# Another split of the first loads over two DMA queues, in a fused linear-attention and MLP kernel

## The chip, the cores and the metric

The kernel runs on one core of a Trainium2 chip. The metric is device time in microseconds (us) of one execution, as the median over several runs. A core has five engines that run their own instruction lists side by side and wait for each other through semaphores: TensorE (PE in the profile, with PEld for its weight loads), VectorE (DVE), ScalarE (ACT), GpSimd (POOL) and SyncE (SP). Data comes from the chip's main memory (HBM) into on-chip memory (SBUF) by DMA: an engine issues a DMA instruction, and 16 DMA engines, shared by all, move the bytes in packets. In this kernel DMAs are issued by POOL (the profile's queue q0, "software_dynamic") and by SP (queue q1, "hardware_dynamic").

## The reference

Eight batches of eight heads, 576 positions, head size 64. Attention with a cosine-weighted feature map, and then a two-layer MLP with a squared ReLU:

```python
theta = np.pi / 2.0 * pos / S
phi(x) = concat([relu(x) * cos(theta), relu(x) * sin(theta)], axis=-1)
q_p, k_p = phi(q), phi(k)
kv = einsum('bhsf,bhsd->bhfd', k_p, v)
z = sum(k_p, axis=2)
num = einsum('bhsf,bhfd->bhsd', q_p, kv)
den = einsum('bhsf,bhf->bhs', q_p, z)[..., None] + 1e-06
x = (num / den) with the heads side by side     # 4608 tokens x 512
h = x @ w_in                                    # 512 x 2048
out = (relu(h) ** 2) @ w_out                    # 2048 x 512
```

All inputs and the output are float32. The matmuls run in bf16.

## The kernel before

A batch has 576 positions. The first 512 are the "main" part: 128 partitions with four positions (j = 0 to 3) each, all heads, 1 MB in float32. The last 64 are the "tail": they are loaded with two DMAs of 64 KB, one for each half of the heads, onto the two halves of the partitions. `load` (lines 61 to 75) issues both, and `piece` (81) gives the part that belongs to a step j; step 4 is the tail. A tile of each of k, v, q and of each tail exists twice (`bufs=2`), so two batches may be on the chip.

For one batch the work is this. `att_k` (192) makes the feature map of k into `kp` (cosine half on VectorE, line 173; sine half on ScalarE, line 183; both scale by columns `cos_col` and `sin_col`). `att_v` (196) casts v to bf16 into `vext`, which has a column of ones so that z comes out of the same matmul. `att_kv` (224) multiplies k by v over all steps (`kz`, line 243). `att_feat` makes the feature map of q (`qp`), `att_qT_pe` (278) transposes it on TensorE (`tq`), `att_num` (301) multiplies it by kv, `att_div` (320) divides, giving x, and `att_x_pe` (349) transposes x. Then `gemm1` (367) multiplies by w_in (`hps`, line 388) in slots, ScalarE applies the ReLU (396), VectorE squares (403), and `gemm2` or `pair_mm` multiplies by w_out.

The order on each engine is written out by hand, inside `tc.manual_schedule()` (742): batch 0's attention stands first by itself, and from line 785 on the slots of the MLP run, with pieces of the next batches' attention hung onto slot numbers (`at`, `plan`). Each engine works through its own list in order. TensorE is kept busy from the start by `warm(34)` (747): 34 matmuls on a tile of zeros, whose result nobody reads; `warm(1)` (770) and `fill` stand further on.

The first loads, in the order of the code: k of batch 0 on POOL with its two tails on SP; `constants()` (92), which on POOL makes an index (`iota`, 99) and the identity matrix and on ScalarE two sine activations for `sin_col` and `cos_col`; v on POOL with its tails on SP; q on POOL in two halves (steps 0 and 1, then 2 and 3) with its tails on SP. Behind the work of batch 0 in the code, but with nothing to hold them on POOL, follow w_in in four pieces (`load_w1`, 117; float32 in HBM, cast to bf16 on the way; piece i holds what slot i of `gemm1` needs), q of batch 1 with its tails, a piece of w_out, k of batch 1, a piece of w_out, v of batch 1, two pieces of w_out, and batch 2.

The scheduler gives POOL's DMAs eight semaphores in turn. A ninth DMA waits at issue until the one that had its semaphore before has landed, and what stands behind it in POOL's list waits too. In the program before, the eight first are k, v, the halves of q and the four pieces of w_in; the next, q of batch 1, waits for k.

Of the kernel before, what the change touches and what calls it, by code (L numbers as in the profile page):

```python
# [11 lines left out]
F32 = mybir.dt.float32  # L12
# [7 lines left out]
def kernel(  # L20
# [9 lines left out]
    nc = tc.nc  # L30
    P = nc.NUM_PARTITIONS
    B, H, S, D = q.shape
# [6 lines left out]
    J = S // P  # L39
    MAIN = J * P  # L40
    TAIL = S - MAIN
    HH = H // 2
# [5 lines left out]
    inp = ctx.enter_context(tc.tile_pool(name="inp", bufs=2))  # L48
# [9 lines left out]

    kqv = {}

    def load(src, nm, b, eng, parts=1, tail_eng=None):
        main = inp.tile([P, H, J, D], F32, name=nm, tag=nm, bufs=2)
        tail = inp.tile([P, HH, D], F32, name=nm + "t", tag=nm + "t", bufs=2)
        for i in range(parts):
            js = slice(i * J // parts, (i + 1) * J // parts)
            eng.dma_start(
                out=main[:, :, js, :],
                in_=src[b, :, 0:MAIN, :].rearrange("h (p j) d -> p h j d", j=J)[:, :, js, :],
            )
        for g in range(2):  # L70
            (tail_eng or eng).dma_start(
                out=tail[g * TAIL : (g + 1) * TAIL, :, :],
                in_=src[b, g * HH : (g + 1) * HH, MAIN:S, :].rearrange("h p d -> p h d"),
            )
        kqv[nm, b] = (main, tail)

    def load_batch(b, eng, order):
        for nm in order:
            load({"k": k, "v": v, "q": q}[nm], nm, b, eng)

    def piece(nm, b, j):
        main, tail = kqv[nm, b]
        return main[:, :, j, :] if j < J else tail[:, :, :]


    ident = const.tile([P, P], BF16, name="ident")
# [5 lines left out]
    def constants():  # L92
        sidx = const.tile([P, J + 1], F32, name="sidx")
        for p0, p1, c, n, base, mult in [
            (0, P, 0, J, 0, J),
            (0, TAIL, J, 1, MAIN, 1),
            (TAIL, P, J, 1, MAIN, 1),
        ]:
            nc.gpsimd.iota(
                sidx[p0:p1, c : c + n],  # L100
                pattern=[[1, n]],
                base=base,
                channel_multiplier=mult,
                allow_small_or_imprecise_dtypes=True,
            )
        bias_pi2 = const.tile([P, 1], F32, name="bias_pi2")
        nc.vector.memset(bias_pi2, math.pi / 2.0)
        theta_scale = (math.pi / 2.0) / S
        nc.scalar.activation(cos_col, sidx, ACTF.Sin, bias=bias_pi2[:], scale=-theta_scale)
        nc.scalar.activation(sin_col, sidx, ACTF.Sin, bias=0.0, scale=theta_scale)  # L110
        make_identity(nc, ident)
# [5 lines left out]
    def load_w1(i, n):  # L117
        f0, f1 = i * DFF // n, (i + 1) * DFF // n
        nc.gpsimd.dma_start(
            out=w1sb[:, :, f0:f1],  # L120
            in_=moe_w_in[:, f0:f1].rearrange("(kb p) f -> p kb f", p=P),
        )

    def load_w2(i, n):
        h0, h1 = i * HB // n, (i + 1) * HB // n
        nc.gpsimd.dma_start(
            out=w2sb[:, h0:h1, :],
            in_=moe_w_out[h0 * P : h1 * P, :].rearrange("(hb p) f -> p hb f", p=P),
        )
# [62 lines left out]
    def att_k(b, j, cos=feat_cos):  # L192
        for f in (cos, feat_sin):
            f(kp_of(b, j), piece("k", b, j), j)

    def att_v(b, j, eng, h0=0, h1=H):
        copy = eng.copy if eng is nc.scalar else eng.tensor_copy
        vx, vxt = vexts[b % 2]
        if j == J:
            copy(out=vxt[:, :, 0:D], in_=piece("v", b, j))  # L200
        else:
            copy(out=vx[:, j, h0:h1, 0:D], in_=piece("v", b, j)[:, h0:h1, :])  # L202

    def warm(n):

        wm = ps_h.tile([P, 2, FP], F32, name="wm", tag="hps", bufs=2)
        for i in range(n):
            nc.tensor.matmul(
                out=wm[:, i % 2, :], lhsT=zeros[:, 0:P], rhs=zeros[:, :], start=True, stop=True
            )  # L210
# [13 lines left out]
    def att_kv(b, part):  # L224
        vx, vxt = vexts[b % 2]
        if part == 0:
            kvzs[b] = att.tile([P, H, E1], BF16, name="kvz", tag="kvz", bufs=2)
            kzs[b] = ps_a.tile([P, 2, FP], F32, name="kz", tag="pa", bufs=1)
        kz = kzs[b]

        for j in (0, 1) if part == 0 else range(2, NS):
            for hh in range(HH):
                for half in range(2):
                    h = half * HH + hh
                    if j < J:
                        lhsT, rhs = kp_of(b, j)[:, h, :], vx[:, j, h, :]
                    else:  # L240
                        p0, p1 = half * TAIL, (half + 1) * TAIL
                        lhsT, rhs = kp_of(b, j)[p0:p1, hh, :], vxt[p0:p1, hh, :]
                    nc.tensor.matmul(  # L243
                        out=kz[:, half, hh * E1 : (hh + 1) * E1],
                        lhsT=lhsT,
                        rhs=rhs,
                        start=(j == 0 and hh == 0),
                        stop=(j == J and hh == HH - 1),
                    )
        if part == 1 and b:  # L250
            att_kvz(b, nc.scalar.copy)

    def att_kvz(b, copy):
        copy(
            out=kvzs[b].rearrange("p (a h) e -> p a (h e)", a=2),
            in_=kzs[b][:, :, 0 : HH * E1],
        )

    def att_feat(b, j, parts="cs"):
        for c in parts:  # L260
            f = feat_cos if c == "c" else feat_sin
            f(qp_of(b, j), piece("q", b, j), j)
# [15 lines left out]
    def att_qT_pe(b, j, apart=False):  # L278

        nh = H if j < J else HH  # L280
        tq = ps_y.tile([P, H, P], BF16, name="tq", tag="yps", bufs=2)
        tqs[b, j] = [tq[:, 0:HH, :]]
        if apart:
            hi = ps_h.tile([P, HH, P], BF16, name="tqh", tag="hps", bufs=2)
            tqs[b, j].append(hi)
        elif nh == H:
            tqs[b, j].append(tq[:, HH:H, :])
        for h in range(nh):
            nc.tensor.transpose(  # L289
                tqs[b, j][h // HH][:, h % HH, :], qp_of(b, j)[:, h, :], ident[:, :]  # L290
            )

    def att_qT_copy(b, j, both=False):
        qpTs[b, j] = []
        for i, tq in enumerate(tqs[b, j]):
            t = att.tile([P, HH, P], BF16, name=f"qpTp{i}", tag=f"qpTp{i}", bufs=3)
            copy = nc.scalar.copy if both and i else nc.vector.tensor_copy
            copy(out=t[:, :, :], in_=tq[:, :, :])
            qpTs[b, j].append(t)
# [363 lines left out]
    for j in (2, 3):  # L663
# [12 lines left out]
        k=(8, 8, 8, 9, 9),  # L676
        f=(4, 5, 6, 12, 13),
        v=(10, 10, 10, 10, 10),
        kv=(11, 11),
        d=(12, 14, 16, 17, 20),  # L680
        t=(5, 6, 7, 16, 19),
# [7 lines left out]
        k=(21, 22, 23, 24, 25),  # L689
# [8 lines left out]
        k=(29, 31, 32, 34, 35),  # L698
# [5 lines left out]
    for b in range(4, B):  # L704
# [5 lines left out]
            k=(o, o, o + 1, o + 1, o + 2),  # L710
# [29 lines left out]
            fn2(*args)  # L740

    with tc.manual_schedule():
        load(k, "k", 0, nc.gpsimd, 1, nc.sync)
        constants()
        load(v, "v", 0, nc.gpsimd, 1, nc.sync)
        load(q, "q", 0, nc.gpsimd, 2, nc.sync)
        warm(34)
        for j in range(NS):
            att_k(0, j)
        att_v(0, 0, nc.vector)  # L750
        att_v(0, 1, nc.scalar)
        att_v(0, 2, nc.vector)
        att_v(0, 3, nc.vector)
        att_v(0, J, nc.vector)
        for i in range(4):
            load_w1(i, 4)
        load_batch(1, nc.gpsimd, "q")
        load_w2(0, 4)
        load_batch(1, nc.gpsimd, "k")
        load_w2(1, 4)  # L760
        load_batch(1, nc.gpsimd, "v")
        for i in range(2, 4):
            load_w2(i, 4)
        load_batch(2, nc.gpsimd, "qkv")
        att_kv(0, 0)
        att_kv(0, 1)
        att_feat(0, 0)
        att_feat(0, 1)
        att_kvz(0, nc.vector.tensor_copy)
        warm(1)  # L770
        for j in range(2):
            att_qT_pe(0, j, True)
        for j in range(2):
            att_qT_copy(0, j, True)
            att_num(0, j, True)
        for j in range(2):
            att_div(0, j)
        att_feat(0, 2, "s")
        att_feat(0, 3, "s")
        for j in range(2):  # L780
            fill(4 - j)
            att_x_pe(0, j, True)
        att_feat(0, 2, "c")
        att_feat(0, 3, "c")
        for s in range(len(slots)):
            run(s)
# [29 lines left out]
```

## Time and profile before

| | |
|---|---|
| median of 6 runs | 289.0 us (288.72 to 290.7) |
| profiled execution, its own time | 289.09 us |
| its span in the profile | 287.3 us |
| busy share of the span: PE, PEld, DVE, ACT, POOL | 97%, 82%, 71%, 56%, 15% |
| chain that ended last | PE 89%, DMA 3%, DVE 2%, ACT 2% |
| read from HBM, written | 36.70 MB, 9.44 MB |
| SP's first DMA issue, POOL's | 0.74 us, 1.29 us |
| warm(34) | 1.19 to 11.04 us |
| first kz matmul, first tq, first hps | 12.36, 14.06, 18.25 us |
| granted TensorE clock, mean | 0.997 |

Times inside the run count from the start of the span. A line of the timeline gives the start, the time taken, the engine, the line of the code, the operation with the tile written and the tiles read, and in brackets how long the engine had been idle and what ended that. "xN" says that N instructions are merged into the line. A DMA instruction's own time is only that of its issue; when the data has landed is seen from who was waiting for it.

### The profile page before, as it was taken

Reading aid. Unit: us, or ns where it says so; the run is one execution under the profiler, and the core shown is the slowest. Engines: PE = TensorE matmul, PEld = TensorE weight load, DVE = VectorE, ACT = ScalarE, POOL = GpSimd, SP = SyncE. Lnnn points to the kernel's source line nnn. Section 1 sums busy time; section 2 is a strip of 40 time slices with the busy share of each in tenths; the row PEclk is TensorE's granted clock in tenths of the full one; section 3 lists DMA queues with packets and bytes.
Section 4 is the critical chain, followed back from the end, with each engine's and each line's share of the span. In section 5 each row is a group of like instructions: output and inputs, shape, how many; then the busy total and the mean of one; then the engine's idle time right before and its main releaser. Section 6 shows DMA issues by size and latency. Waiting matters only on the chain.

```text
span 287.3 us, 7337 instructions
## 1 busy us (share of the span) xinstructions
PE 279.9 (97%) x3070; PEld 235.9 (82%) x3070; DVE 204.6 (71%) x457; ACT 161.7 (56%) x245; POOL 42.1 (15%) x70
## 2 busy tenths in 40 slices
PE   8899999999999999999999999999999999999995
PEld 3479845888678888889988888888988888889884
DVE  0767664688698499787598776977677877546585
ACT  2675743579759769445881448834695461155210
POOL 8633506650000000000002000000000000000002
PEclk9999999999999999999999999999999999999998
DMA  6999995999468899999429985499809620300014
GB/s 184 334 206 289 323 264 201 364 363 276 76 99 205 184 258 229 234 327 186 147 95 205 344 158 164 124 252 285 230 3 232 118 46 3 141 7 2 0 75 146
DMA packets 74497, 53.04 MB, mean 185 GB/s; under 512 B 52032, under 2 KB 68928, under 8 KB 74464
## 3 DMA queue, kind: packets, MB, share of 16 engines
q1 hardware_dynamic: 63840, 26.09, 40.2%
q0 software_dynamic: 10480, 26.35, 30.2%
q8 instruction: 24, 0.39, 0.6%
q10 hardware_dynamic: 144, 0.13, 0.1%
q14 instruction: 9, 0.07, 0.1%
HBM read 36.70 MB, written 9.44 MB: 161 GB/s over the span
## 4 chain that ended last, share of the span: by engine, by line
PE 89%; DMA 3%; DVE 2%; ACT 2%; issue 1%; POOL 1%; POOLq 0%; ACTq 0%
PE hps L388 42%; PE ya L530 9%; PE yc L530 9%; PE yu L530 7%; PE yv L530 5%; PE num L315 4%; PE kz L243 3%; DMA v<-in_v_dram 3%; PE yps L461 2%; PE yps L437 2%; PE yh L437 2%; PE tq L289 1%; DVE ysb L542 1%; DVE u L542 1%; PE tx L356 1%
## 5 line engine op out<-in xcount | busy, mean ns | idle before, releaser
L388 PEld LDWEIGHTS <-w1sb 128*128 128x128 bf16 x1344 | 113.4, 98 | 12.4 <-issue 2.0
L388 PE MATMUL hps<-xT,w1sb 128*128 128x256 bf16 (+1 forms) x1088 | 119.3, 266 | 0.7 <-ACT rt L396 0.2
L396 ACT ACTIVATE rt<-hps 128x1024 bf16<-128x1024 f32 x72 | 73.6, 1023 | 67.1 <-PE hps L388 44.8
L403 DVE TENSOR_TENSOR gT<-rt 128x1024 bf16<-128x1024 bf16 x64 | 44.0, 687 | 20.1 <-ACT rt L396 20.1
L530 PEld LDWEIGHTS <-gs 128*128 128x128 bf16 x480 | 46.8, 98 | 5.4
L415 POOL DMA_DIRECT2D out_dram<-ysb x14 | 7.5, 539 | 171.6 <-DVE ysb L542 144.9
L530 PEld LDWEIGHTS <-gT 128*128 128x128 bf16 x312 | 29.8, 98 | 3.5
L183 ACT ACTIVATE kp<-k,sin_col 128x512 bf16<-128x512 f32 x32 | 22.4, 717 | 4.3 <-DMA k<-in_k_dram 4.3
L329 DVE TENSOR_TENSOR x<-num,rden 128x512 bf16<-128x512 f32 x32 | 22.1, 691 | 1.1
L183 ACT ACTIVATE qp<-q,sin_col 128x512 bf16<-128x512 f32 x32 | 22.0, 720 | 0.8 <-DMA q<-in_q_dram 0.8
L325 DVE TENSOR_SCALAR den<-num 128x8 f32<-128x8 f32 (+1 forms) x40 | 6.6, 164 | 21.2 <-PE num L315 21.1
L526 DVE TENSOR_TENSOR gs<-gT 128x1024 bf16<-128x1024 bf16 x26 | 17.8, 685 | 0.0
L530 PE MATMUL ya<-w2t,gs 128*128 128x256 bf16 x120 | 15.6, 273 | 0.0
L530 PE MATMUL yu<-w2t,gs 128*128 128x256 bf16 x120 | 15.6, 273 | 0.0
L530 PE MATMUL yc<-w2sb,gs 128*128 128x256 bf16 x120 | 15.6, 273 | 0.0
L388 PE MATMUL hps<-xTt,w1sb 128*128 128x128 bf16 x256 | 15.1, 219 | 0.2 <-ACT rt L396 0.2
L173 DVE TENSOR_SCALAR kp<-k,cos_col 128x512 bf16<-128x512 f32 x21 | 10.7, 533 | 6.1 <-DMA k<-in_k_dram 6.1
L173 DVE TENSOR_SCALAR qp<-q,cos_col 128x512 bf16<-128x512 f32 x32 | 15.0, 495 | 0.1
L202 ACT CAST vext<-v 128x512 bf16<-128x512 f32 x23 | 14.1, 614 | 1.4 <-DMA v<-in_v_dram 1.4
L530 PE MATMUL yu<-w2sb,gs 128*128 128x256 bf16 x112 | 14.5, 273 | 0.0
L581 ACT COPY s<-yu 128x256 f32<-128x256 f32 x14 | 5.2, 372 | 15.3 <-PE yu L530 15.3
L530 PE MATMUL yc<-w2sb,gT 128*128 128x256 bf16 x104 | 13.5, 273 | 0.0
(98 smaller groups left out, 338.6 us busy)
## 6 DMA issues: line engine op xcount, KB each, us to landing
out_dram<-ysb POOLq DMA_DIRECT2D x14, 512.0 KB, 4.2
k<-in_k_dram POOLq DMA_DIRECT2D x4, 1024.0 KB, 8.0
v<-in_v_dram POOLq DMA_DIRECT2D x4, 1024.0 KB, 8.7
k<-in_k_dram SPq DMA_DIRECT2D x4, 1024.0 KB, 7.2
v<-in_v_dram SPq DMA_DIRECT2D x4, 1024.0 KB, 8.5
q<-in_q_dram SPq DMA_DIRECT2D x4, 1024.0 KB, 5.8
q<-in_q_dram POOLq DMA_DIRECT2D x3, 1024.0 KB, 12.2
w1sb<-in_moe_w_in_dram POOLq DMA_DIRECT2D x4, 512.0 KB, 13.7
```

Source lines behind the costliest of these rows:

```text
L173: nc.vector.tensor_scalar(out=dst[:, :, 0:D], in0=src, scalar1=0.0, scalar2=cos_col[:, j : j + 1], op0=ALU.max, op1=ALU.mult,)
L183: nc.scalar.activation(out=dst[:, :, D:F], in_=src, func=ACTF.Relu, scale=sin_col[:, j : j + 1])
L202: copy(out=vx[:, j, h0:h1, 0:D], in_=piece("v", b, j)[:, h0:h1, :])
L243: nc.tensor.matmul(out=kz[:, half, hh * E1 : (hh + 1) * E1], lhsT=lhsT, rhs=rhs, start=(j == 0 and hh == 0), stop=(j == J and hh == HH - 1),)
L315: nc.tensor.matmul(out=out, lhsT=lhsT, rhs=kvz[:, half * HH + hh, :], start=True, stop=True)
L329: nc.vector.tensor_tensor(out=x_of(b, j).rearrange("p (b k) (l d) -> p b k l d", b=n, l=2), in0=n4[:, :, :, 0:D].rearrange("p b (k l) d -> ...
L388: nc.tensor.matmul(out=out, lhsT=w1sb[:, kb, hb * P : (hb + 1) * P], rhs=rhs, start=(kb == 0), stop=(kb == KB - 1),)
L396: nc.scalar.activation(out=rt[:, :, :], in_=hps[:, :, :], func=ACTF.Relu)
L403: nc.vector.tensor_tensor(out=dst, in0=rt[:, :, :], in1=rt[:, :, :], op=ALU.mult)
L437: nc.tensor.matmul(out=ypss[b][tt], lhsT=gTs[b][:, hb, tt * P : (tt + 1) * P], rhs=w2sb[:, hb, :], start=(hb == 0), stop=(hb == HB - 1),)
L526: nc.vector.tensor_tensor(out=t[:, :, :], in0=in0, in1=in1, op=op)
L530: nc.tensor.matmul(out=acc, lhsT=lhs[:, hb, :], rhs=rhs[:, hb, :], start=(hb == 0), stop=(hb == HB2 - 1),)
```

## The change

`load` is split in two: `load_main` for the first 512 positions and `load_tail` for the last 64, each with one queue. `load_batch`, which serves batches 1 to 7, calls both in turn and issues what it issued before. For batch 0 the order of the first loads is new:

- k's main part is issued by SP, and nothing else is: the six tail DMAs that SP had are gone from its list.
- POOL issues k's tail (two DMAs), v, v's tail (two), then makes its part of the constants, and then issues the halves of q.
- q's tail (two DMAs) is issued by POOL behind the four pieces of w_in and ahead of q of batch 1.
- `warm(34)` becomes `warm(31)`.

With the eight semaphores in turn, POOL's first eight DMAs are now k's two tails, v, v's two tails, the halves of q and the first piece of w_in. The second and the third piece of w_in wait for k's tails, the fourth for v, the two tails of q for v's tails, and q of batch 1 for the first half of q. The compute instructions of VectorE and ScalarE are the same, in the same order; TensorE's list loses three warm matmuls.

```diff
-    def load(src, nm, b, eng, parts=1, tail_eng=None):
+    def load_main(src, nm, b, eng, parts=1):
         main = inp.tile([P, H, J, D], F32, name=nm, tag=nm, bufs=2)
-        tail = inp.tile([P, HH, D], F32, name=nm + "t", tag=nm + "t", bufs=2)
         for i in range(parts):
             js = slice(i * J // parts, (i + 1) * J // parts)
             eng.dma_start(
                 out=main[:, :, js, :],
                 in_=src[b, :, 0:MAIN, :].rearrange("h (p j) d -> p h j d", j=J)[:, :, js, :],
             )
+        kqv[nm, b] = main
+
+    def load_tail(src, nm, b, eng):
+        tail = inp.tile([P, HH, D], F32, name=nm + "t", tag=nm + "t", bufs=2)
         for g in range(2):
-            (tail_eng or eng).dma_start(
+            eng.dma_start(
                 out=tail[g * TAIL : (g + 1) * TAIL, :, :],
                 in_=src[b, g * HH : (g + 1) * HH, MAIN:S, :].rearrange("h p d -> p h d"),
             )
-        kqv[nm, b] = (main, tail)
+        kqv[nm + "t", b] = tail
...
     with tc.manual_schedule():
-        load(k, "k", 0, nc.gpsimd, 1, nc.sync)
+        load_main(k, "k", 0, nc.sync)
+        load_tail(k, "k", 0, nc.gpsimd)
+        load_main(v, "v", 0, nc.gpsimd)
+        load_tail(v, "v", 0, nc.gpsimd)
         constants()
-        load(v, "v", 0, nc.gpsimd, 1, nc.sync)
-        load(q, "q", 0, nc.gpsimd, 2, nc.sync)
-        warm(34)
+        load_main(q, "q", 0, nc.gpsimd, 2)
+        warm(31)
...
         for i in range(4):
             load_w1(i, 4)
+        load_tail(q, "q", 0, nc.gpsimd)
         load_batch(1, nc.gpsimd, "q")
```

More of the change, by code (lines that the diff above doesn't have):

```diff
@@ L74, in load @@
             )
-        kqv[nm, b] = (main, tail)
+        kqv[nm + "t", b] = tail
     def load_batch(b, eng, order):
         for nm in order:
-            load({"k": k, "v": v, "q": q}[nm], nm, b, eng)
+            for part in (load_main, load_tail):
+                part({"k": k, "v": v, "q": q}[nm], nm, b, eng)
     def piece(nm, b, j):
-        main, tail = kqv[nm, b]
-        return main[:, :, j, :] if j < J else tail[:, :, :]
+        return kqv[nm, b][:, :, j, :] if j < J else kqv[nm + "t", b][:, :, :]
     ident = const.tile([P, P], BF16, name="ident")
```

## The prediction

> **What bounds the kernel now.** Read first the page: PE is busy 97% of the span and holds 89% of the chain that ended last, so a gain must come from the head, where the tensor engine is not yet fed. Read next the chain of waits in order of time; columns are start, length (us) and what:
>
> ```profile
> 3.51 8.34 DMA v<-in_v_dram
> ...
> 11.87 0.44 DVE vext L202
> ...
> 12.36 1.36 PE kz L243 x40
> 13.72 0.32 PE wm L208
> ...
> 14.06 0.40 PE tq L289 x4
> ```
>
> The head waits for v to land at 11.85, casts it, multiplies k by v (kz), then transposes q (tq). The ScalarE timeline (start, length, operation, in brackets the idle time before it and its releaser) shows that three landings stand close together:
>
> ```profile
> 7.55 2.56 ACT L183 ACTIVATE kp<-k,sin_col 128x512 bf16<-128x512 f32 x4 [4.27 <-DMA k<-in_k_dram]
> 11.87 0.62 ACT L202 CAST vext<-v 128x512 bf16<-128x512 f32 x1 [1.36 <-DMA v<-in_v_dram]
> 13.29 1.33 ACT L183 ACTIVATE qp<-q,sin_col 128x512 bf16<-128x512 f32 x2 [0.79 <-DMA q<-in_q_dram]
> ```
>
> k lands at 7.5, v at 11.85, the first half of q at 13.27; tq starts 0.77 after q, and kz with one warm matmul ends at the same moment (14.04). So v and q bind together, k has slack. What sets the landings is read from the DMA view of 4 to 12 us (queue, packets, MB, share of 16 engines):
>
> ```profile
> q0 software_dynamic: 643, 2.47, 85.3%
> q1 hardware_dynamic: 1087, 0.26, 14.8%
> ```
>
> The shares sum to 100%: the engines are full, so bytes in front decide. q0 is POOL's queue, q1 SP's. After the head, the w_in pieces bind almost as hard (POOL and PE timelines):
>
> ```profile
> 25.08 0.76 POOL L126 DMA_DIRECT2D w2sb<-in_moe_w_out_dram  x1 [1.92 <-DMA w1sb<-in_moe_w_in_dram]
> 25.14 1.03 PE L388 MATMUL hps<-xT,w1sb 128*128 128x256 bf16 x8
> ```
>
> POOL was released by the fourth w_in piece at about 25.05, and PE's first matmul on it starts at 25.14.
>
> **The change, part by part.** *Prices of bytes.* On q0, 85.3% of 8 us is 6.82 us for 2.47 MB: 0.362 MB per us. So a 1.05 MB main takes 2.90 us, half of q 1.45. On q1 the four tail DMAs of v and q took 14.8% of 8 us, 1.18 us: 0.59 for a pair of tails (0.13 MB), where q0's rate would take 0.36. A main on q1 is seen at 205.2 to 207.2 us: 0.75 MB at a 106.4% share, 2.13 us, so 2.98 us for k.
>
> *Bytes before the first half of q.* Before: k 2.90, v 2.90, half q 1.45, three pairs of tails 1.77, sum 9.02 us. After: k 2.98, v 2.90, half q 1.45, two pairs of tails on POOL 0.72, sum 8.05, since q's tail goes behind w_in. That is 0.97 less. The start of the stream stays: SP's first issue is at 0.74 in both, and the first packets come at 2.2. From 2 to 4 us the share is 57.6%, so of the 1.8 us after 2.2 some 0.65 stay empty; a quiet main on SP (203.7 to 205.2) fills 60.9%, leaving 0.59, and now k's tail (0.36) falls into that hole. I take 0.3 for it, bounds 0 and 0.36. q moves by 0.97 + 0.3 = 1.27, to 12.0; tq by the same, to 12.79. Bounds: if tails cost on POOL what they cost on SP (0.59), 0.5; if the start-up hole closes wholly (0.65), 1.6.
>
> *v and kz.* In front of v's end: before 2.90 + 2.90 + 1.77 = 7.57, after 2.98 + 2.90 + 0.36 = 6.24, so v moves by 1.33 + 0.3 = 1.6, to 10.25. kz starts 0.49 later (12.36 against 11.87), 10.74, ends 12.10, and with the warm matmul 12.44: 0.35 before q lets tq go. q decides.
>
> *warm 34 to 31.* Three warm matmuls at 0.213 us end the block at 10.40 instead of 11.04. I cost this at nothing: kz is hidden behind q. With 34, kz would run 11.04 to 12.40 and tq could go at 12.74, still under 12.79. If that cover is gone, it is worth 0.3.
>
> *k alone on SP.* One issue replaces six (SP's next work is at 62.9), and starts 0.55 before POOL's did. The quiet case at 202.55 landed 5.4 us after issue, which gives 6.1; the median of k on SP, 7.2 us with its own tails and other traffic, gives 7.9. What follows k on VectorE: four kp (2.78) and kpt, casts 3.07 after the landing, 1.34 of casts, then qp and 0.77 to tq: k's landing + 5.2. To stay behind q's 12.79, k must land by 7.6. I take 6.1 because k is on the engines alone at first; with 7.9 the gain shrinks to 0.9.
>
> *POOL's order.* POOL's first DMA starts at 1.29. Now two kt issues (1.25), v (0.94), two vt (1.25), and 0.15 because a first issue took 1.05 and not 0.90: 4.88. The constants follow, which took 2.35 to 3.49: the last iota ends at 5.40, the cosine table 0.33 later, the sine table at 5.83. kp needs them; k's landing at 6.1 hides them by 0.3. q's halves issue at 6.05, 1.6 later than at 4.46. POOL's first k packets came at 3.0, 1.7 after issue, so q's can come at 7.75, while v's bytes last until about 9: hidden, with 1.3 to spare. The w_in pieces issue at 7.8 to 10.15 for three of them; POOL keeps eight DMAs in flight, and with four tails among them the fourth piece waits for v's landing, 10.25, where it went at 8.4. Queued behind it are q's two tails, q of batch 1, the w_out pieces and batch 1's k and v. Three w_in pieces of 2.55 us (the spacing of their landings: 17.3, 19.95, 22.5, 25.05) and q are ahead in the stream, so it is covered for over 8 us.
>
> *What is late next.* The w_in pieces move by the same 1.27 as q, and PE by 1.27: the 0.09 us of margin at 25.14 stays, and caps the gain at what the stream gives. Behind w_in, q's tails add 0.36, so q of batch 1 comes 0.9 earlier only: it released POOL at 27.93, PE's need (VectorE qp at 28.75) moves by 1.27, and 0.4 of slack is left. q's own tail is read at 40.69. From 18.25 PE runs without a wait of length (after 40 us the list of waits gives it 0.4 us), so the shift passes to the end.
>
> *Sum.* Span 287.3 - 1.27 = 286.03. Outside the span lie 289.09 - 287.3 = 1.79: 287.82. The profiled run stands 0.09 above the median 289.0, so 287.7 is my number; bounds 0.5 and 1.6 give 287.4 to 288.5.
>
> **A rule against it.** Rows first: while both queues were flowing the engines gave each about as many packets, whatever their size. From 8.5 to 11.5 us (256-byte tails against 4-KB packets), and from 164.25 to 165.25 (v's 1-KB packets on SP against the result's on POOL):
>
> ```profile
> q0 software_dynamic: 265, 1.02, 92.3%
> q1 hardware_dynamic: 249, 0.06, 9.2%
> ```
>
> ```profile
> q0 software_dynamic: 81, 0.33, 80.9%
> q1 hardware_dynamic: 80, 0.08, 21.9%
> ```
>
> But where SP's DMA was under way first, POOL's barely came through, at 157 to 159.5:
>
> ```profile
> q1 hardware_dynamic: 500, 0.51, 79.2%
> q0 software_dynamic: 23, 0.04, 4.3%
> ```
>
> and 580 against 28 at 6.5 to 7.25. The Trainium skill, "DMA: Bandwidth & Descriptors", section "Queues, rings and completion order", says that each engine takes turns between the queues it has work for, a packet at a time. By that rule alone k would get a fifth of the bytes once v starts, and the sum would be the first rival's, 294.0. The last two rows differ from the rule, and k starts before v, so I forecast by them, but not by much.
>
> **The rivals.** *First, slower: k is outrun on its own queue.* v's packets can come from 2.69 + 1.7 = 4.4. By then k has had 2.2 us: 0.27 MB in the first 1.5 (seen at 203.7 to 205.2), then 0.25, less up to 0.13 for its tail: 0.39 to 0.52. The rest, 0.53 to 0.66 MB, at the 0.08 MB per us of 164.25, takes 6.6 to 8.2 us, and POOL has v, v's tail and q (2.2 MB at 0.33, 7 us) and then w_in to keep it up. k lands at 11.0 to 12.6, say 11.9; tq at 17.1, 3.0 late. Also PE idles from 10.4 until k + 3.5 = 15.4, 5 us. At the end the granted clock was at 0.5 some 2.1 us after the last matmul (283.8), and at the start warm matmuls were 0.43 apart until 5.9, 4.7 us after the first. PE's pieces of the chain in such a stretch (kz, warm, tq, num, fills) are about 4 us; doubled they add 0 (hidden) to 4: 2. Sum: 289.0 + 3.0 + 2 = 294.0, bounds 291 to 297. It decides from a k landing past 8.9 (14.06 - 5.2).
>
> The Trainium skill, "TensorE: Matmul & The Clock Gate", section "Part 1: The HAM clock gate", puts the relapse at an idle window of about 3.4 us; no idle stretch of PE inside this trace is that long, so it shows neither for nor against (after the warm block the idle time is 1.32).
>
> *Second, no change: shared halfway.* POOL's packets stay scarce for 1 us (as at 6.5 to 7.25) and then go one for one: k has 0.2 to 0.33 MB left at 5.4, 2.5 to 4.1 us more, landing 7.9 to 9.5, tq 13.1 to 14.7: 288.0 to 289.6, 288.8 in the middle. For it: both kinds of rows occur. Against: v's and k's tails arrive on POOL ahead and open its queue at 2.8.
>
> **How the numbers follow.** Forecast 0.58, first rival 0.32, second 0.10. A difference under 0.3% (0.87 us: 288.1 to 289.9) can't be told from none. Of the forecast, 0.05 lies above 288.1. Faster 0.53, same 0.15, slower 0.32. The likeliest case's own range is 287.4 to 288.5. The whole range goes from 287.2 (0.03 below) to 294.0, which leaves half of the first rival out: 0.19 outside.
>
> **What would show it.** Right: kp starts at about 6.1, vext at 10.3, tq at 12.8, the first hps at 17.0, w_in's pieces 1.3 earlier each. Wrong: kp starts after 8.9, v lands before k, and in 4.4 to 10 us the two queues show like numbers of packets; then the warm block is followed by a PE gap of over 3 us. If q lands at 12 but hps does not move, w_in held it.

## The result, and the profile after

| kernel | median us | runs | ratio to before (95%) |
|---|---|---|---|
| before | 289.07 (288.66 to 290.7) | 48 | |
| changed | 287.92 (287.21 to 294.24) | 22 | 0.996 [0.9949, 0.997] |

The change is worth 1.15 us, 0.4%; the interval goes from 0.3% to 0.5%. Two executions of the changed kernel were disturbed (294.24 us, and the first profiled one with 294.11) and are left out of the ratio, so the lines below are from another execution of the same program (`again`: 288.01 us, span 286.2). The page's line numbers have moved by 3 against before.

ScalarE's timeline in the head (start, length, operation, idle time before and its releaser) is read against the three landings shown of before, 7.55, 11.87 and 13.29:

```profile
6.24 2.56 ACT L186 ACTIVATE kp<-k,sin_col 128x512 bf16<-128x512 f32 x4 [0.47 <-DMA k<-in_k_dram]
9.48 0.62 ACT L205 CAST vext<-v 128x512 bf16<-128x512 f32 x1 [0.28 <-DMA v<-in_v_dram]
10.98 1.34 ACT L186 ACTIVATE qp<-q,sin_col 128x512 bf16<-128x512 f32 x2 [0.88 <-DMA q<-in_q_dram]
```

All three are earlier: k by 1.31, v by 2.39, q by 2.31. The DMA view of 2 to 4 us and then of 4 to 8 us shows where that comes from (queue, packets, MB, share of the 16 engines). First before:

```profile
q1 hardware_dynamic: 540, 0.13, 28.8%
q0 software_dynamic: 27, 0.11, 28.8%
```

and the changed kernel in the same 2 us:

```profile
q1 hardware_dynamic: 488, 0.50, 90.4%
```

By 4 us 0.50 MB have moved instead of 0.24; by 8 us, with 1.55 against 1.29 MB more, the lead is 0.52 MB. SP's queue carries k's first packets at 1.86 and the engines are full from 3 us on (104% from 3 to 4), while POOL's k came in at 3.2.

The end moved by less than the head. TensorE's timeline shows what took the place of the landing of q:

```profile
11.76 0.40 PE L292 MATMUL tq<-ident,qp 128*128 128x128 bf16 x4 [0.29 <-ACT qp L186]
...
16.56 1.96 PE L391 MATMUL hps<-xT,w1sb 128*128 128x128 bf16 x32 [0.45 <-DMA w1sb<-in_moe_w_in_dram]
...
21.59 1.92 PE L391 MATMUL hps<-xT,w1sb 128*128 128x256 bf16 x16 [0.19 <-DMA w1sb<-in_moe_w_in_dram]
...
24.20 1.92 PE L391 MATMUL hps<-xT,w1sb 128*128 128x256 bf16 x16 [0.22 <-DMA w1sb<-in_moe_w_in_dram]
```

The first tq is 2.30 us earlier (14.06 before), the first hps 1.69 (18.25), the fourth slot's hps only 0.94 (25.14). In between, the tensor engine now waits three times for w_in; before it waited for it not once. The chain of waits (start, length, what) says the same: it no longer runs over v and kz, but over POOL's issues and the landing of the fourth w_in piece (the 13.61 us are its time in the queue behind q and the three pieces ahead of it).

```profile
5.97 2.02 POOL q L65 x2
8.00 2.54 POOL w1sb L122 x3
10.54 13.61 DMA w1sb<-in_moe_w_in_dram
24.20 1.92 PE hps L391 x16
```

One figure makes all later runs readable: from the fourth slot's first hps to the end of the span it takes the same time wherever PE meets no long wait further on. Before: 287.3 - 25.14 = 262.2; here 286.2 - 24.20 = 262.0. So a program's place is told by the start of its fourth slot.

### The profile page after: what moved, and what is told of

Its sections match the earlier page's. It is cut to its first block, busy times and chain, and to the rows that moved or that the text cites. A ratio compares the mean times of both kernels' runs of the same rounds, so it can differ in the third digit from the quotient of the medians.

```text
span 292.3 us, 7327 instructions
## 1 busy us (share of the span) xinstructions
PE 281.9 (96%) x3067; PEld 236.6 (81%) x3067; DVE 204.7 (70%) x457; ACT 161.9 (55%) x245; POOL 45.5 (16%) x75
## 4 chain that ended last, share of the span: by engine, by line
PE 81%; DMA 11%; POOL 3%; DVE 2%; ACT 1%; issue 1%; POOLq 0%; ACTq 0%
PE hps L391 38%; PE ya L533 9%; PE yc L533 9%; PE yu L533 7%; DMA qpT<-qp 6%; DMA w1sb<-in_moe_w_in_dram 5%; PE yv L533 4%; PE num L318 3%; PE yps L440 2%; PE kz L246 2%; PE yh L440 2%; PE yps L464 2%; DVE ysb L545 1%; PE tq L292 1%; POOL w1sb L122 1%
## 5 line engine op out<-in xcount | busy, mean ns | idle before, releaser
L318 PEld LDWEIGHTS <-qpT 128*128 128x128 bf16 (+1 forms) x240 | 10.5, 102 | 6.7 <-DMA qpT<-qp 3.9
L318 PE MATMUL num<-kvz,qpT 128*128 128x65 bf16 (+1 forms) x240 | 12.2, 198 | 3.4 <-DMA qpT<-qp 3.4
L176 DVE TENSOR_SCALAR qp<-q,cos_col 128x512 bf16<-128x512 f32 x32 | 14.9, 492 | 0.0
```

The source lines that it names most:

```text
L176: nc.vector.tensor_scalar(out=dst[:, :, 0:D], in0=src, scalar1=0.0, scalar2=cos_col[:, j : j + 1], op0=ALU.max, op1=ALU.mult,)
L318: nc.tensor.matmul(out=out, lhsT=lhsT, rhs=kvz[:, half * HH + hh, :], start=True, stop=True)
```

## The experiments

The theory after this result: k on SP feeds the DMA engines earlier, all that follows in the stream comes earlier, and w_in's landing caps what reaches the end. Its rivals: that the moves of the tails, not of k, brought the time; that the order or cut of the bytes has more to give; and, for the forecast's own first rival, that k was never in danger of being outrun.

### One part alone

`again` is the changed kernel once more, on the chip of the next three.

> The changed kernel as it is, for a profile to compare with before. Both theories: 287.9 us. Head: kp from 6.3, vext 9.7, tq 12.2, first hps 16.3 to 16.4 (1.9 earlier than before), but the third and fourth piece of w_in hold PE for about 0.25 us each, so that the fourth slot of gemm1 starts only 1.3 us earlier than before. If instead hps of the fourth slot is 1.9 earlier and the time is lost later, something behind the head gave 0.8 back.

Measured: 288.24 us (10 runs), 0.9964 [0.9949, 0.9979], against 289.02 for before (33 runs): 0.78 us. The fourth slot came 0.94 us earlier and not 1.3, and the first hps 1.69 and not 1.9.

`qt_late` is the kernel before with nothing changed but q's tail, which goes to POOL behind w_in:

```diff
-        load(q, "q", 0, nc.gpsimd, 2, nc.sync)
+        load(q, "q", 0, nc.gpsimd, 2, None, False)
...
             load_w1(i, 4)
+        load_tail(q, kqv["q", 0][1], 0, nc.gpsimd)
```

> Before, with nothing changed but q's tail, which goes from SP to POOL behind w_in. Theory 'bytes in front' (what counts is how much lies ahead of q and w_in on the full DMA engines): 0.59 us less ahead of v, q and w_in, so 288.4 to 288.5. Rival 'start' (the gain comes from k's earlier start on a queue of its own): no change, 289.0.

Measured: 289.05 us (12 runs), 0.9991 [0.9978, 1.0004]. The first tq came at 13.67 instead of 14.06, the fourth slot at 24.75 instead of 25.14: 0.39 us in one profile, which the times don't resolve from nothing.

`k_sp` is the kernel before with k's main part on SP, ahead of the six tails that stay there:

```diff
-        load(k, "k", 0, nc.gpsimd, 1, nc.sync)
+        load(k, "k", 0, nc.sync)
```

> Before, with nothing changed but k's main part, which SP issues ahead of the six tails. Bytes in front: the bytes ahead of w_in are as before, only the empty 0.65 us of the start shrinks: 288.6 to 288.8, and v's and q's tails, queued behind k on SP, may come late. Start: k lands at 6.3 as in the changed kernel and nearly the whole gain is there, 288.0.

Measured: 290.51 us (12 runs), 1.0045 [1.0025, 1.0066], slower, so both lines of the expectation failed. k was as early as in the changed kernel (kp at 6.47), but from 6.5 to 12 us the DMA view shows the tails behind k on SP beside v and q on POOL:

```profile
q0 software_dynamic: 490, 1.86, 92.1%
q1 hardware_dynamic: 486, 0.12, 9.7%
```

The two queues get equal numbers of packets, and SP's tails have 256 bytes in each while POOL's have 4 KB. So v's tail is outrun. The waits of 9 to 18 us (engine, tile, line of this kernel, releaser, total, times, longest) show what it cost:

```profile
PE kz L243 <- DVE vextt L200: 2.5, 1, 2.5
...
DVE vextt L200 <- DMA vt<-in_v_dram: 2.4, 1, 2.4
```

v's tail landed at 14.4, the first tq came at 15.72, and it ran at 0.63 us for four matmuls instead of 0.40: the granted clock was 0.50 from 15 to 20 us. The profiled run is the slowest of the twelve (292.79 us). Six runs, this one among them, had a mean granted clock of 0.988 to 0.994 and took 290.8 to 292.8 us; in the other six it was 1.0, and they took 289.5 to 290.2. So the fall of the clock came in half of the runs, and the program is slower without it too.

`k_pool` is the changed kernel with k's main part put back on POOL, ahead of the tails, and nothing on SP:

```diff
-        load_main(k, "k", 0, nc.sync)
+        load_main(k, "k", 0, nc.gpsimd)
```

> The changed kernel with k's main part on POOL ahead of k's tail, so SP issues nothing at the head. Bytes in front: the same bytes as in the changed kernel, but the stream starts at 3.0 (POOL's first packets before) and not at 2.0: 0.6 to 1.0 slower than the changed kernel, 288.5 to 288.9. Start: all of the gain is gone, 289.0 or more, since POOL also issues one DMA more ahead of v.

Measured: 289.08 us (12 runs), 1.0005 [0.9984, 1.0025]: with the tails moved and k not, no gain is seen, and the interval leaves 0.5 us at most. Between 2 and 4 us only 0.13 MB moved, less than before (0.24), since POOL's first packet comes at 3.0 us here, as it came at 3.2 before:

```profile
q0 software_dynamic: 32, 0.13, 45.5%
```

Its profile stands higher than its median (290.46) for a reason told below.

Neither part does it alone: k on SP needs the tails off SP, or they are outrun; the tails on POOL need k on SP, or the stream starts late.

### Order and slack

Four variants of the changed kernel. `v_first` puts v ahead of k's tails on POOL:

```diff
         load_main(k, "k", 0, nc.sync)
-        load_tail(k, "k", 0, nc.gpsimd)
         load_main(v, "v", 0, nc.gpsimd)
+        load_tail(k, "k", 0, nc.gpsimd)
```

> The changed kernel with v's main part ahead of k's tails in POOL's list, so v is issued at 1.3 and not at 2.7. Theory 'first come': what SP issued first goes through before POOL's packets flow (in the changed kernel POOL's first packet came at 5.0, although issued at 1.3): k lands at 6.2 to 6.4 as before, v 0.2 earlier, time as the changed kernel, 287.7 to 288.3. Rival 'turns, packet by packet': v's 4-KB packets come from 3.0 and k gets one 1-KB packet for each: k lands after 9 and the time is 289 to 294.

Measured: 287.77 us (6 runs), 0.9953 [0.9937, 0.9969]. v was issued at 1.3 us, yet from 2 to 5 us the DMA view of this run has one queue only:

```profile
q1 hardware_dynamic: 855, 0.88, 97.3%
```

No packet of v passed while k, which had begun first, kept the engines full. In the order that the forecast's first rival was made for, `again`, the view of the same window has SP's queue alone too (864 packets), and POOL's first packet came at 5.1 us, when k was nearly through.

`qt_early` loads q's tail right behind q instead of behind w_in:

```diff
         load_main(q, "q", 0, nc.gpsimd, 2)
+        load_tail(q, "q", 0, nc.gpsimd)
...
-        load_tail(q, "q", 0, nc.gpsimd)
         load_batch(1, nc.gpsimd, "q")
```

> The changed kernel with q's tail on POOL right behind q's halves, ahead of w_in. Bytes in front: w_in's pieces come 0.3 to 0.5 later (0.36 at POOL's rate; in the run with the late tail alone they came 0.5 earlier), and since PE waits for them, so does the end: 288.3 to 288.6. If w_in does not set the pace behind the head, no difference from the changed kernel.

Measured: 288.18 us (12 runs), 0.9968 [0.9953, 0.9983]. In the changed kernel, the late place of q's tail is worth nothing that can be measured.

`w34` gives the three warm matmuls back (`warm(31)` becomes `warm(34)`).

> The changed kernel with 34 warm matmuls again. The prediction costs the cut at nothing, since q and then w_in set the pace: as the changed kernel, 287.7 to 288.3, although kz may start later by up to 0.6. Rival: the cut is part of the gain, 288.5.

Measured: 288.19 us (7 runs), 0.9971 [0.9957, 0.9985]. Its profile tells more than its time, since in this execution v landed at 10.84 and not at 9.48:

```profile
13.31 0.40 PE L292 MATMUL tq<-ident,qp 128*128 128x128 bf16 x4 [0.16 <-ACT qp L186]
...
24.39 1.91 PE L391 MATMUL hps<-xT,w1sb 128*128 128x256 bf16 x16
```

tq was 1.55 us later than in `again` and the fourth slot only 0.19 (and `v_first`, with tq at 13.22, had it at 24.29). Without any wait for w_in the way from tq to the fourth slot takes 24.39 - 13.31 = 11.08 us, the same as before (25.14 - 14.06). So the fourth slot starts at the later of two times: tq + 11.08, or the landing of the fourth w_in piece, 24.15 in `again`. In these two profiles with a slow head tq decides (the piece had landed at 24.2 in `w34` and at 23.7 in `v_first`); in the quick head of `again` w_in does.

`kv_early` changes the order in which POOL loads batches 2 and 3 (q's tail of batch 2 behind k and v; batch 3 as k, v, q), to move traffic away from 62 to 72 us.

> The changed kernel with other places in POOL's list for the loads of batches 2 and 3: q's main, k and v of batch 2 ahead of q's tail of batch 2 (which waits at 33 to 44 us until batch 0's tail of q has been read, and holds all behind it), and k and v ahead of q for batch 3. The DMA engines are then fed in 35 to 44 us, and POOL's stream is through before SP's transposes at 62 us start: they take 4 to 6 us and not 9 to 18. If the transposes beside POOL's stream are what scatters the times, the median comes to 287.2 to 287.7 with a narrower spread; if w_in alone sets it, the median is the changed kernel's.

Measured: 288.07 us (7 runs), 0.9961 [0.9946, 0.9975]: no different. The transposes took 8.96 us and not 4 to 6, so the edit did not bring about what it was meant to, and its theory stays untested. Why it was tried: in the first profile of the changed kernel SP's two transposing DMAs of batch 2 took 17.90 us. SP's timeline there, and then TensorE's:

```profile
61.52 17.90 SPq L275 DMA_TRANSPOSE qpT<-qp  x2
```

```profile
79.88 0.62 PE L318 MATMUL num<-kvz,qpT 128*128 128x65 bf16 x8 [3.39 <-DMA qpT<-qp]
```

PE waited 3.39 us and the granted clock was 0.50 from 80 to 84. In other profiles the same pair took 8.7 us (before), 8.95 (`again`), 8.96 (`kv_early`), 12.5 (`qt_late`), 10.6 (`k_sp`), 14.9 (`split23`) and 15.9 (`k_pool`, where PE waited 1.0 us). The length varies with and without the change, and what sets it stayed open.

### Cutting w_in

If PE waits for whole w_in pieces, smaller ones should let it start. `split23` loads the third and fourth piece as two halves each, `split_all` loads w_in in eight pieces:

```diff
-        for i in range(4):
-            load_w1(i, 4)
+        for i in range(8):
+            load_w1(i, 8)
```

> The changed kernel with the third and the fourth w_in piece each loaded as two halves. If the stream of w_in sets what the change gains, because a slot needs its whole piece, then the first halves of these two land some 1.2 us earlier than the whole pieces, the waits of the hps matmuls for w_in in the third and fourth slot (0.19 and 0.22 us of 0.86) go, and the time falls by 0.2 to 0.6 us: 287.6 to 288.0. If the head sets it, or if the shorter rows slow the stream, the fourth slot starts at 24.2 or later and the time is 288.2 or more.

Measured: 288.44 us (287.02 to 289.51, 12 runs), 0.9974 [0.9957, 0.999].

> The changed kernel with all of w_in loaded in eight pieces. If the whole pieces are what the slots wait for, all three waits of hps for w_in go (0.45, 0.19 and 0.22 us), the first hps starts at 16.1 and the fourth slot's at 23.4, and the time is 287.4 to 287.8. If the stream's bytes set it, the fourth slot's hps matmuls meet a wait inside the slot and the time stays at 288.2; four more issues on POOL (0.6 us each) and shorter rows could make it 288.6.

Measured: 288.19 us (7 runs), 0.9969 [0.9958, 0.9981]. TensorE's timeline of `split_all`:

```profile
12.67 0.40 PE L292 MATMUL tq<-ident,qp 128*128 128x128 bf16 x4 [0.41 <-ACT qp L186]
...
23.87 1.91 PE L391 MATMUL hps<-xT,w1sb 128*128 128x256 bf16 x16
```

The waits for w_in are gone, as the theory had it, but the time did not follow, because the head is the other bound and was at 12.67 here and at 13.36 in `split23`: with nothing else to wait for, the fourth slot comes 11.2 to 11.3 us after tq, at 23.87 and at 24.62. Half of the expectation failed: w_in was a bound, but not the only one.

`vf_split` joins `v_first` and `split_all`.

> The two edits that gave the lowest medians or took the waits for w_in away, together: v ahead of k's tails on POOL, and w_in in eight pieces. If the head and the w_in stream bind about equally and each edit eases another one of them, the time falls below either alone: 287.3 to 287.7, ratio 0.994. If the bytes of the stream bind whatever their order and cut, the time stays with the others: 287.8 to 288.3, ratio 0.996.

Measured: 287.82 us (9 runs), 0.9959 [0.9946, 0.9971]; its profile has the shortest span of all, 285.6, with tq at 12.21 and the fourth slot at 23.59. Its interval covers that of the changed kernel, so no version was found that beats it.

### The rival's mechanism, called up

`k_behind` puts 0.13 MB ahead of k on SP, v's two tails, and begins POOL's list with v:

```diff
+        load_tail(v, "v", 0, nc.sync)
         load_main(k, "k", 0, nc.sync)
-        load_tail(k, "k", 0, nc.gpsimd)
         load_main(v, "v", 0, nc.gpsimd)
-        load_tail(v, "v", 0, nc.gpsimd)
+        load_tail(k, "k", 0, nc.gpsimd)
```

> The changed kernel with v's two tails issued by SP ahead of k, and POOL beginning with v and then k's tails. If a transfer that is under way first goes through and the later queue has to wait, SP's 0.13 MB of tails and 1.05 MB of k pass before POOL's v, k lands at 6.9 to 7.6, kp starts there and the time is 288.0 to 288.8. If what counts is that the two queues take turns by packet, v's 4-KB packets outrun k's 1-KB ones as soon as POOL's queue has opened at 4 to 5 us, k lands at 9 to 12, the first tq comes after 14.1 and the time is 289.5 to 293.

Measured: 294.99 us (4 runs), 1.0204 [1.0189, 1.022]: slower by 5.9 us, more than either line had expected. SP could issue k only at 2.18, and v had been issued at 1.29. The DMA view of 5 to 6.5 us, of 6.5 to 10, and of 10 to 12:

```profile
q0 software_dynamic: 135, 0.55, 101.2%
q1 hardware_dynamic: 10, 0.01, 1.6%
```

```profile
q1 hardware_dynamic: 808, 0.83, 69.0%
q0 software_dynamic: 150, 0.42, 33.3%
```

```profile
q0 software_dynamic: 172, 0.64, 83.1%
q1 hardware_dynamic: 157, 0.15, 22.2%
```

At first v holds k back as k had held v back in `v_first`. As v runs out, most of the packets are k's. What is left of k by 10 us, 0.21 MB, then goes packet for packet beside POOL's larger ones (0.15 MB against 0.64 in 2 us). k landed at 14.3. TensorE's timeline, and the busy times and clock of 16 to 20 us (window, length, busy time and instructions of each engine, then clock, DMA share and GB/s):

```profile
16.72 0.60 PE L246 MATMUL kz<-vext,kp 128*128 128x65 bf16 x8 [6.87 <-DVE vext L205]
...
20.04 0.63 PE L292 MATMUL tq<-ident,qp 128*128 128x128 bf16 x4 [0.33 <-issue]
```

```profile
16.00:20.00 4.00, 2.41 (x40) 2.17 (x41) 2.58 (x9) 3.08 (x6) 1.97 (x2) 0.50 1.24 207
```

The tensor engine stood idle 6.87 us, came back at half clock, and the fourth slot started at 31.71: 31.71 + 261.9 = 293.6, the span. So the mechanism that the forecast feared is real. `v_first` differs from this program only in where v's tails go: with nothing in front of it on its queue k escapes, with 0.13 MB in front of it it does not.

## Why the prediction was right, and where its terms were not

*The number.* 287.7 was forecast, with 287.4 to 288.5 as the likeliest case's own range; 287.92 was measured. The sum of 1.27 us stands against 1.15, and against 0.78 in `again` on another chip. That they agree is in part luck: the parts of the sum erred in both directions, and so did the way from q to the end.

*The sum's two terms were mis-sized, in opposite directions, as far as single profiles tell.* The tails' term, 0.97, looks too large. `qt_late` moved tq by 0.39 where one pair was priced at 0.59. `k_pool` makes every move of a tail and keeps k on POOL; it starts its stream 0.11 MB, or 0.30 us, behind that of before, so the term would have left about 0.7 at tq, and 0.25 came. `qt_early` put a pair back in front of w_in, and w_in landed no later (23.7 us against 24.15 in `again`). The start-up term, 0.3 with 0.36 as its upper bound, was too small: 0.26 MB of lead at 4 us, at the forecast's own 0.362 MB per us, is 0.72 us, and 0.53 if tails and k on SP are priced as the forecast did. How the gain divides between the two is not shown, since v's landing alone scatters by 1.4 us. The step of the sum that failed is "The start of the stream stays". It took its measure from the share of 60.9% that a quiet main on SP showed at 203.7 to 205.2 us; here k filled 90.4% from 2 to 4 us, and its packets came at 1.86 instead of 2.2.

*k on SP.* Forecast to land at 6.1 by the quiet case, 7.9 by the median; kp started at 6.14 to 6.49 in every run in which k stood first on SP. It decides from 8.9, so the first rival was far off in the changed kernel.

*The rule against it.* The Trainium skill, "DMA: Bandwidth & Descriptors", section "Queues, rings and completion order", has each engine take turns between the queues with work, a packet at a time. Taken for the packets of the profile, `k_sp` (490 against 486) agrees with it, `v_first` (855 to none in 3 us) does not, and `k_behind` shows both in turn. The section's packet holds several descriptors, up to 64; whether a packet of the profile is such a one or a part of it no run shows, so `v_first`, with 53 to each engine, speaks against the rule only in the first case. Weighing the row in which SP's queue was under way first (500 to 23) above the rule was right; the condition it stood on, that k starts before v, is what `k_behind` takes away. The rival's price for k outrun was 294.0, bounds 291 to 297; `k_behind`, with k's start pushed back, came to 294.99, though there k landed at 14.3 and not at 11.9.

*v, q, the first hps.* Forecast 10.3, tq 12.8 and hps 17.0. v and tq fell at 9.48 and 11.76 in `again`, at 10.84 and 13.31 in `w34`, which has the same loads in the same order; the first hps came between 16.34 and 17.50. The forecasts lie inside that spread, which they did not foresee.

*w_in and the cap.* "The 0.09 us of margin ... caps the gain at what the stream gives" was the decisive sentence: the cap was there, but both of its numbers were off. The forecast read the fourth landing from POOL's release, 25.05, and POOL is released some 0.28 us after a piece has landed. The view of w_in's tile has the issues (first and last) and the times to landing, before and then in `again`:

```profile
L119 POOL DMA_DIRECT2D w1sb<-in_moe_w_in_dram x4: 777/785/800, 6.2 to 8.4; - x4
DMA to landing us min/median/max: 10.9/13.7/16.4
```

```profile
L122 POOL DMA_DIRECT2D w1sb<-in_moe_w_in_dram x4: 760/838/926, 8.0 to 10.5; - x4
DMA to landing us min/median/max: 8.5/11.0/13.6
```

The fourth piece is the last issued and the longest on its way. It landed at 8.4 + 16.4 = 24.8 before, 0.34 us ahead of PE, and at 24.15 in `again`. So w_in came 0.65 us earlier where 1.27 was forecast (0.6 to 1.1 in the other profiles with four pieces, where it landed at 23.7 to 24.2). A margin nearly four times as wide as thought made up for part of that: 0.65 + 0.34, less the 0.05 that PE still starts behind the landing, is the 0.94 to which a head 2.3 us earlier was held in `again`. Why the stream's lead of 0.52 MB at 8 us reached w_in only in part stays open. The fourth piece was to wait for v's landing to be issued. In `again` it did not (issued at 10.54, v landed by 9.48), in `w34` POOL waited 0.70 us for it. It was covered as forecast: the third piece ended a wait of PE at 21.59 in `again`.

*POOL's order and constants.* The sine column was forecast for 5.83 and was made at 5.77, the halves of q were to issue at 6.05 and issued at 5.96: hidden, as was said. POOL's first packets of k had come at 3.2 before and not at 3.0, which takes 0.2 from the 1.3 us to spare.

*warm 34 to 31.* Costed at nothing; `w34` measures no difference, since q decides tq and not kz.

*Behind 18.25.* "PE runs without a wait of length, so the shift passes to the end" held, with 262.0 us from the fourth slot on, except where the transposes of batch 2 took too long. That wait was in no step of the forecast.

*Second rival.* Shared halfway, 288.8: not seen; kp started at 6.14 to 6.49, and k was to land at 7.9 to 9.5.

## What to carry to other kernels

When the head of a kernel waits for its loads, look at what the DMA engines move in the first microseconds. Here it paid to put the first big transfer alone on the queue that starts earliest (k on SP, packets from 1.86 us), with nothing in front of it (`k_behind`) and nothing small behind it that is needed soon (`k_sp`). In these runs the transfer under way first went through, and where both queues flowed they shared by packet, so the queue with small packets lost. When a head gets shorter, look for the next stream that binds (here w_in): the gain at the end is what that stream lets through. Read a landing from the DMA's own time to landing, not from the engine that happens to be released by it.

## What the runs showed of the hardware

- One queue shut the other out: v, issued at 1.3 us on POOL, had no packet through by 5 us while k ran on SP (855 to 0 in `v_first`); in `k_behind` v did the same to k (135 to 10 from 5 to 6.5 us).
- SP's queue moved 0.50 MB by 4 us (`again`), POOL's alone 0.13 (`k_pool`).
- The granted clock fell to 0.50 in the profile of `k_sp` with no idle stretch above 2.50 us: two stretches, 1.25 and 2.50 us, with 1.1 us of kz between them, were enough. The Trainium skill, "TensorE: Matmul & The Clock Gate", section "Part 1: The HAM clock gate", gives an idle window of about 3.4 us as the condition; the stretches of 3.39 us (the first profile of the changed kernel) and 6.87 us (`k_behind`) agree with that, `k_sp` does not if the window must be wholly idle.
- The clock records of the traces put this down to steps. In `k_sp` the clock rose at 4.07, fell at 14.31 and rose at 21.14, which is three and two times 3.413 us apart; in the profile of before it rose at 5.96 and fell at 285.85, 82 times 3.413. The step that ends with the fall held 1.13 us of matmuls in `k_sp` (10.90 to 14.31), 0.87 in the first profile of the changed kernel (75.62 to 79.03) and 1.34 at the end of before (282.44 to 285.85); after a step with 1.58 us (`k_behind`, 8.27 to 11.68) it stayed up.
- v's landing differed by 1.4 us between executions with the same loads (9.48 and 10.84), though the bytes moved by 8 us were nearly the same (2.05 and 1.93 MB, a third of a microsecond of stream). Its cause stayed open.
